# A two-dimensional Fourier transform followed by an MLP: the start of the program in finer pieces and another order

## The chip, the core and the metric

The kernel runs on one core of a Trainium2 chip. The metric is device time in microseconds (us) of one execution; three executions of the kernel before took 1763.95, 1764.96 and 1766.8 us, a median of 1764.96 us. The engines are named as the profile names them: PE is TensorE (matmul), DVE is VectorE, ACT is ScalarE, POOL is GpSimd, SP is SyncE, which here only issues DMAs.

## The reference

```python
def _attn_ref(x):                       # x: (8, 3008, 256)
    X = np.fft.fft(x, axis=1)
    X = np.fft.fft(X, axis=2)
    return X.real.astype(np.float32)
...
def _moe_ref(x, w_in, w_out, s, b):     # x: (24064, 256), w_in: (256, 2048), w_out: (2048, 256)
    h = x @ w_in
    r = np.maximum(h, 0.0)
    g = s * (r * r) + b
    return (g @ w_out).astype(np.float32)
```

The real part of a two-dimensional Fourier transform of each of eight batch items is taken; the result, as 24064 rows of 256 values, goes through an MLP with 2048 hidden units whose activation is the squared ReLU, scaled by `s` and shifted by `b`.

## The kernel before, in words

**The work.** The transform along the sequence is done as matmuls with tables of cosines and sines (`transform`, in two phases for a batch item); the transform along the 256 features is folded into the first weight matrix, so that the MLP's first layer reads the spectrum of the sequence directly. By symmetry only half of the columns is computed: 1506 for a batch item, in 3 blocks of 502. For every block the hidden units go through in 16 groups of 128. One group of one block is a **step**: 8 x 3 x 16 = 384 steps in all. A step has two halves.

- `first_layer` (L637): 6 matmuls into a two-bank PSUM tile `ab` (L643), then three VectorE instructions that add the term of the Nyquist feature (column `wny` times the row `ebc`) and form the sum and the difference for the two mirrored columns (L645 to L647, tile `h`), then on ScalarE ReLU, square (L648, L649) and a rounding cast to `gh` (L272), then on GpSimd the rest, `gl = h - gh` (L273). `split` (L270) is the helper that makes a high and a low part; every product of the kernel is made of three matmuls over such parts (high x high, high x low, low x high).
- `second_layer` (L659): 12 matmuls (L666) of `gh` and `gl` with the second weights `wo_h`, `wo_l` into four PSUM tiles `po`, which gather over the 16 steps of a block. `finish` (L671) scales them and writes them out.

**The start.** Before the first step can run, the first batch item has to be loaded, folded and transformed, and the weights have to be read. The letters of the table `START` each stand for one piece of a Python generator, which issues instructions up to its next `yield`:

- `x` and `y` (`load_first`, `load_second`): fold the eight tiles of the first item; the tables X_ON_VECTOR and Y_ON_VECTOR say for which tiles the work of a piece (L508 and L512, or L522 to L524) goes to VectorE instead of GpSimd.
- `s` and `u` (`transform(0, 0)`, `transform(0, 1)`): the two phases of its transform. A `pair` (L564) is 16 matmuls, then a copy out of PSUM (L579; by FIRST_COPIES_ON_SCALAR on ScalarE or VectorE) and VectorE sums (L580, L584, L585). Each phase ends in `store`, which casts the result into the blocks `spec_h` (ScalarE, L545) and takes the rest into `spec_l` (GpSimd, L547).
- `r`, `a`, `b`, `e`: the weights come as 64-bit floating-point numbers and are decoded in 16 parts. `r` issues the load of a part, `a` runs two ScalarE instructions (L308, L310), `b` three VectorE ones (L313 to L315), and `e` a GpSimd addition (L318), followed, for the eight parts of the second weights, by the `split` into `wo_h` (ScalarE) and `wo_l`.
- `w` (`fold_w_in`, L329): one of four foldings of the first weights: matmuls in float32 (L337; the profile counts eight), then a ScalarE copy of the Nyquist row (L341), the split into `wd_h` and `wd_l`, and two DMAs on SP (L343, L344) that write the row to DRAM and read it back as a column of `wny`. A folding serves four steps.
- `n` and `m` (`nyquist`): the transform of the Nyquist feature, stored to DRAM and read back as `ebc`.
- `t`: the load of the transform's tables.
- `L` and `S`: `first_layer` and `second_layer` of the next step. `l`, `v` and `o`: load and transform of the second batch item, for later steps.

**What sets the order.** The instructions of TensorE, VectorE, ScalarE and GpSimd are chained in the order in which they are issued (`_in_order`, L236): each engine executes its own list strictly in that order, and an instruction that waits holds up all behind it. DMAs on SP are outside of that chain. `START` covers 57 first halves and 54 second halves; from there on the table `BATCH` is run over and over, a string of letters for the 48 steps of one batch item and the load and transform of the next.

**Buffers.** The tiles `h`, `gh` and `gl` have three buffers each, `ab` two, the weight loads two (they use the buffers of the first two input tiles); at the start the input tiles 2 to 7 lie in the buffers of `gl` and `gh`, so that the first steps need these tiles folded.

Of the kernel before, what the change touches and what calls it, by code (L numbers as in the profile page):

```python
# [9 lines left out]
F32 = mybir.dt.float32  # L10
# [5 lines left out]
P = 128  # L16
NB, S, D, FF = 8, 3008, 256, 2048
# [4 lines left out]
G = 24  # L22
NL = 4 * G
NK = H + 2
NT = 502
# [11 lines left out]

LOWS_ON_VECTOR = (3, 5)  # L40
Y_ON_VECTOR = (0, 7)
X_ON_VECTOR = (1, 2, 3, 4, 6)
FIRST_COPIES_ON_SCALAR = (1, 2, 3, 4, 5)
COPIES_ON_SCALAR = ()
SUMS_ON_SCALAR = ()
LOADS = "xxfxxxwxwxx"
# [2 lines left out]
    ("in", 2, 1), ("out", 3), ("in", 3, 0), ("out", 4), ("in", 3, 1), ("out", 5), ("out", 6), ("out", 7),  # L49
)  # L50
START = (
# [6 lines left out]
)  # L58
BATCH = (
# [191 lines left out]
def kernel(ctx: ExitStack, tc: tile.TileContext, xq, xn, dft, turn, feat, w_in, w_out, s, b, out):  # L251
    nc = tc.nc
# [17 lines left out]
    def split(hi, lo, src, lo_engine):  # L270

        nc.scalar.copy(hi, src)  # L272
        lo_engine.tensor_sub(lo, src, hi.bitcast(F32))  # L273
# [9 lines left out]
    wny = const.tile([P, NJ], F32, name="wny")  # L283
# [19 lines left out]
    def decode(part, raw, aux):  # L303

        low, high = raw[:, :, 0], raw[:, :, 1]
        magnitude, bits = aux[:, 0], aux[:, 1]
        rest, w = magnitude.bitcast(F32), bits.bitcast(F32)
        nc.scalar.activation(rest, high.bitcast(F32), AF.Abs)  # L308

        nc.scalar.activation(low, low.bitcast(mybir.dt.uint32), AF.Copy, scale=2.0 ** -29)  # L310
        yield

        nc.vector.tensor_scalar(rest, rest, 2.0 ** -15, None, ALU.max)  # L313
        nc.vector.tensor_scalar(bits, magnitude, 3, 0x3FFFFFFF, ALU.logical_shift_left, ALU.bitwise_and)
        nc.vector.scalar_tensor_tensor(bits, high, -(1 << 30), bits, ALU.bitwise_and, ALU.bitwise_or)  # L315
        yield

        nc.gpsimd.tensor_add(bits, bits, low)  # L318
        if part[0] == "out":
            at = slice(2 * part[1], 2 * part[1] + 2)  # L320
            split(
                wo_h[:, at], wo_l[:, at], w.rearrange("p (j d) -> p j d", j=2),
                nc.vector if part[1] in LOWS_ON_VECTOR else nc.gpsimd,
            )
        else:
            halves[part[1:]] = w, rest
        yield

    def fold_w_in(f):  # L329

        (w0, row), (w1, _) = (halves[f, c] for c in range(2))
        row = row[0:1]
        at = slice(f * 512, (f + 1) * 512)
        ps = two_banks()
        for kind in range(2):
            for c, w in enumerate((w0, w1)):
                nc.tensor.matmul(  # L337
                    ps[:, kind], feat_sb[:, c, kind * P:(kind + 1) * P], w, start=c == 0, stop=c == 1
                )
        yield  # L340
        nc.scalar.copy(row, ps[0:1, 1])  # L341
        split(wd_h[:, :, at], wd_l[:, :, at], ps, nc.vector)
        nc.sync.dma_start(wny_dram[:, at], row)  # L343
        nc.sync.dma_start(wny[:, 4 * f:4 * f + 4], wny_dram[0, at].rearrange("(j p) -> p j", p=P))  # L344
        yield


# [289 lines left out]
    def first_layer(su, blk, j, ebc):  # L637
        mh, ml = block_of(su, blk)
        ps = two_banks()[:, :, :NT]
        fj = slice(j * P, (j + 1) * P)  # L640
        for kind in range(2):
            for i, (w, m) in enumerate(((wd_h, mh), (wd_h, ml), (wd_l, mh))):
                nc.tensor.matmul(ps[:, kind], w[:, kind, fj], m[:, kind], start=i == 0, stop=i == 2)  # L643
        h = act.tile([P, 2, NT], F32, name="h")
        nc.vector.scalar_tensor_tensor(h[:, 0], ebc, wny[:, j:j + 1], ps[:, 0], op0=ALU.mult, op1=ALU.add)  # L645
        sub(h[:, 1], h[:, 0], ps[:, 1])  # L646
        add(h[:, 0], h[:, 0], ps[:, 1])  # L647
        nc.scalar.activation(h, h, AF.Relu)  # L648
        nc.scalar.activation(h, h, AF.Square)  # L649
        gh = act.tile([P, 2, NT + 2], F32R, name="gh")  # L650
        gl = act.tile([P, 2, NT + 2], F32R, name="gl")
        if (su, blk) == (0, 0):

            nc.gpsimd.memset(gh[:, 0, NT:].bitcast(F32), 1.0)
            nc.gpsimd.memset(gl[:, 0, NT:].bitcast(F32), 0.0)  # L655
        split(gh[:, :, :NT], gl[:, :, :NT], h, nc.gpsimd)
        return gh, gl

    def second_layer(po, j, g, sums):  # L659
        gh, gl = g  # L660
# [76 lines left out]
    def go_on():  # L737
        for i in range(len(WORDS)):
            next(decoding[i])
            yield  # L740

    def fold_weights():
        for f in range(4):
            yield from fold_w_in(f)

    pending = []
    po = None
    ebc = None
    step = 0
# [1 line left out]
    def first():  # L751
        nonlocal ebc, step
        su, blk, j = step // (NBLK * NJ), step // NJ % NBLK, step % NJ
        step += 1
        if j == 0:
            ebc = small.tile([P, NT], F32, name="ebc")
            for ph in range(2):
                first, last = max(0, blk * NT - SPLIT * ph), min((blk + 1) * NT - SPLIT * ph, e_dram[ph].shape[1])
                if first < last:
                    at = first + SPLIT * ph - blk * NT  # L760
                    nc.sync.dma_start(
                        ebc[:, at:at + last - first], e_dram[ph][su, first:last].partition_broadcast(P)
                    )
        pending.append(((su, blk, j), first_layer(su, blk, j, ebc)))

    def second():
        nonlocal po
# [6 lines left out]

    work = {
        "t": tables(), "x": load_first(tiles), "y": load_second(tiles), "r": load_weights(), "a": begin_weights(),
        "b": go_on(), "e": go_on(), "w": fold_weights(),
        "n": nyquist(0, t_ny, room, room_r), "m": nyquist(1, t_ny, room, room_r),
        "s": transform(0, 0), "u": transform(0, 1), "l": load(1),
        "v": transform(1, 0), "o": transform(1, 1),  # L780
# [1 line left out]
    for what in START.split():  # L782
        if what == "L":
            first()
        elif what == "S":
            second()
        else:
            next(work[what])

    su = 1  # L790
    while step < NB * NBLK * NJ:
        work = {}
        if su < NB - 1:
            work = {"l": load(su + 1), "v": transform(su + 1, 0), "o": transform(su + 1, 1)}
        for what in BATCH.split():
            if what == "L" and step < NB * NBLK * NJ:
                first()
            elif what == "S" and pending:
                second()
            elif what in work:  # L800
                next(work[what])
        su += 1
# [35 lines left out]
```

## Time and profile before

| | us |
|---|---|
| median of three runs | 1764.96 |
| the profiled execution | 1766.39 |
| its span, first to last instruction | 1764.3 |
| PE busy in the span | 1683.20 |
| DVE busy | 1417.67 |
| ACT busy | 1285.81 |
| POOL busy | 953.85 |

A line of a timeline has the start in us, the duration in us, the engine, the line of the program, the operation, output and input tiles, and shapes; in square brackets stands how long the engine sat idle before it and what ended that. A line of a table of stages has the stretch, its length, and for each engine the busy us and the number of instructions, then the granted PE clock (1.00 is full speed), the share of DMA and the GB/s. A group's line has the count, the busy us, the mean in ns, and the idle time before.

### The profile page before, as it was taken

What the parts mean: (1) busy time and instruction counts of PE and PEld (TensorE: products, weight loads), DVE (VectorE), ACT (ScalarE), POOL (GpSimd) and SP (SyncE); (2) the same over time, 40 slices, a digit from 0 to 9 for tenths busy, and PEclk for the clock granted to TensorE, in tenths of its full rate; (3) what the DMA queues carried; (4) which work ended last, traced back from release to release, by engine and by line L of the source; (5) the groups of instructions that cost most, each with busy time, mean ns of one, the idle gap of its engine ahead of it and who ended that gap; (6) DMA issues with size and microseconds to landing.
All of it is one profiled execution on the core that took longest, in us unless ns stands there. A gap on an engine that the chain in (4) does not pass through costs nothing.

```text
span 1764.3 us, 21595 instructions
## 1 busy us (share of the span) xinstructions
PE 1683.2 (95%) x7537; PEld 1386.7 (79%) x7537; DVE 1417.7 (80%) x2145; ACT 1285.8 (73%) x1356; POOL 953.8 (54%) x550
## 2 busy tenths in 40 slices
PE   2687999999999999999999999999999999999998
PEld 1465778888888888888888888888888888888887
DVE  6779987889787997879878897879978798785554
ACT  2565677777778778777777777787787778787776
POOL 4555446555556555564565555565565555555554
PEclk9798999999999999999999999999999999999999
DMA  6321200011000200002000110002100020000000
GB/s 154 94 66 51 81 18 24 30 42 60 30 1 30 75 27 30 21 22 80 16 24 30 42 60 30 5 26 75 30 27 30 19 65 26 5 30 7 24 24 24
DMA packets 26100, 68.57 MB, mean 39 GB/s; under 512 B 5444, under 2 KB 10404, under 8 KB 25896
## 3 DMA queue, kind: packets, MB, share of 16 engines
q1 hardware_dynamic: 25464, 64.84, 11.9%
q0 software_dynamic: 528, 2.36, 0.6%
q8 instruction: 59, 0.97, 0.2%
q14 instruction: 49, 0.40, 0.1%
HBM read 42.46 MB, written 24.73 MB: 38 GB/s over the span
## 4 chain that ended last, share of the span: by engine, by line
PE 84%; DVE 8%; issue 1%; ACT 1%; DVEq 0%; ACTq 0%
PE po L666 54%; PE ab L643 27%; PE ab L573 2%; DVE h L645 1%; DVE h L646 1%; PE ab L574 1%; DVE h L647 1%; DVE xt L493 1%; DVE cs L498 1%; DVE xt L495 0%; DVE lf L352 0%; DVE xt L494 0%; DVE o L683 0%; DVE cs L497 0%; DVE fl L561 0%
## 5 line engine op out<-in xcount | busy, mean ns | idle before, releaser
L273 POOL TENSOR_TENSOR gl<-h,gh 128x1004 fp32r<-128x1004 f32 x384 | 842.2, 2193 | 749.6 <-ACT gh L272 530.0
L648 ACT ACTIVATE h<-h 128x1004 f32<-128x1004 f32 x384 | 400.3, 1042 | 362.7 <-DVE h L647 356.2
L666 PE MATMUL po<-gh,wo_h 128*128 128x502 f32 (+1 forms) x1536 | 484.8, 396 | 0.2
L645 DVE SCALAR_TENSOR_TENSOR h<-ebc,wny,ab 128x502 f32<-128x502 f32 x384 | 281.1, 732 | 246.9 <-PE ab L643 233.7
L666 PE MATMUL po<-gh,wo_l 128*128 128x502 f32 (+1 forms) x1536 | 477.8, 393 | 0.0
L666 PE MATMUL po<-gl,wo_h 128*128 128x502 f32 (+1 forms) x1536 | 476.9, 392 | 0.9 <-POOL gl L655 0.8
L649 ACT ACTIVATE h<-h 128x1004 f32<-128x1004 f32 x384 | 401.3, 1045 | 12.2
L272 ACT CAST gh<-h 128x1004 fp32r<-128x1004 f32 x384 | 397.4, 1035 | 12.4 <-PE po L666 0.3
L666 PEld LDWEIGHTS po<-gl,wo_h 128*128 128x128 f32 x1536 | 292.2, 190 | 61.6 <-POOL gl L655 1.8
L666 PEld LDWEIGHTS po<-gh,wo_l 128*128 128x128 f32 x1536 | 291.1, 189 | 61.9
L666 PEld LDWEIGHTS po<-gh,wo_h 128*128 128x128 f32 x1536 | 289.1, 191 | 60.3 <-DVE o L683 2.6
L643 PE MATMUL ab<-spec_h,wd_h 128*128 128x502 f32 x768 | 304.1, 396 | 27.9 <-DVE h L647 11.7
L643 PE MATMUL ab<-spec_h,wd_l 128*128 128x502 f32 x768 | 301.5, 393 | 3.1 <-DVE wd_l L273 3.1
L643 PE MATMUL ab<-spec_l,wd_h 128*128 128x502 f32 x768 | 300.0, 391 | 0.0
L647 DVE TENSOR_TENSOR h<-h,ab 128x502 f32<-128x502 f32 x384 | 260.5, 678 | 13.2
L646 DVE TENSOR_TENSOR h<-h,ab 128x502 f32<-128x502 f32 x384 | 260.2, 678 | 13.2
L643 PEld LDWEIGHTS ab<-spec_h,wd_h 128*128 128x128 f32 x768 | 146.0, 190 | 65.3 <-DVE h L647 16.8
L643 PEld LDWEIGHTS ab<-spec_h,wd_l 128*128 128x128 f32 x768 | 145.2, 189 | 33.6 <-DVE wd_l L273 3.5
L643 PEld LDWEIGHTS ab<-spec_l,wd_h 128*128 128x128 f32 x768 | 146.2, 190 | 28.9 <-issue 0.2
L573 PE MATMUL ab<-dft_sb,fh 96*128 96x192 f32 x256 | 63.5, 317 | 29.5 <-DMA dft_sb<-in_dft 19.2
L573 PEld LDWEIGHTS ab<-dft_sb,fh 96*128 96x128 f32 x256 | 51.6, 202 | 32.4 <-issue 19.2
L683 DVE TENSOR_SCALAR o<-po,sb_s,bias 128x502 f32<-128x502 f32 x94 | 68.8, 793 | 8.7 <-PE po L666 8.7
(93 smaller groups left out, 987.9 us busy)
## 6 DMA issues: line engine op xcount, KB each, us to landing
xt<-in_xq SPq DMA_DIRECT2D x64, 384.0 KB
out<-o SPq DMA_DIRECT2D x46, 502.0 KB
raw<-in_w_in SPq DMA_DIRECT2D x8, 512.0 KB
raw<-in_w_out SPq DMA_DIRECT2D x8, 512.0 KB
ebc<-e_dram SPq DMA_DIRECT2D x16, 251.0 KB
dft_sb<-in_dft POOLq DMA_DIRECT2D x2, 576.0 KB, 13.2
dft_sb<-in_dft POOLq DMA_DIRECT2D x1, 1152.0 KB, 7.4
ebc<-e_dram SPq DMA_DIRECT2D x8, 126.0 KB
```

What stands on the lines that cost most here:

```text
L272: nc.scalar.copy(hi, src)
L273: lo_engine.tensor_sub(lo, src, hi.bitcast(F32))
L493: add(t[:, 0::2], t[:, 0::2], t[:, 1::2])
L573: nc.tensor.matmul(ps[:, kind, i], fh[:, row, at], tab, start=True, stop=False)
L643: nc.tensor.matmul(ps[:, kind], w[:, kind, fj], m[:, kind], start=i == 0, stop=i == 2)
L645: nc.vector.scalar_tensor_tensor(h[:, 0], ebc, wny[:, j:j + 1], ps[:, 0], op0=ALU.mult, op1=ALU.add)
L646: sub(h[:, 1], h[:, 0], ps[:, 1])
L647: add(h[:, 0], h[:, 0], ps[:, 1])
L648: nc.scalar.activation(h, h, AF.Relu)
L649: nc.scalar.activation(h, h, AF.Square)
L666: nc.tensor.matmul(po[2 * pm + dh][:, :n], l[:, j, dh * P:(dh + 1) * P], r[:, pm, :n], start=start and first, stop=stop and last,)
L683: nc.vector.tensor_scalar(o[:, dh], po[2 * pm + dh][:, :NT], *args, ALU.mult, ALU.add)
```

## The change

**Finer pieces.** The decoding of a weight part has one `yield` more: the GpSimd addition stays with `e`, and the split of the second weights becomes a piece of its own, `f`. The folding of the first weights is cut into three pieces instead of two (the matmuls of the cosine half, those of the sine half, the split). `first_layer` becomes a generator as well: `L` ends with the cast to `gh`, and the subtraction that makes `gl` is a piece `G` of its own. For some of the steps of the first block the table LOWS_OF_STEPS_ON_VECTOR moves that subtraction from GpSimd to VectorE: its entries are 0 to 3, 8, 9, 10, 12 and 13, nine steps. In `BATCH` the subtraction follows the cast directly and stays on GpSimd, as before.

**Another placement.** The `wo_l` split is on VectorE for one part instead of two; the second-half folding `y` is on VectorE for five tiles instead of two; of the first item's eight copies out of PSUM three are on ScalarE instead of five.

**Another order.** `START` is a new string with the same numbers of steps (57 first halves, 54 second halves).

**The first Nyquist weights.** For the first folding, eight small products (weights as the stationary side, one column of the feature table as the moving side) give the Nyquist row directly as a column; one ScalarE copy of 128 x 4 values brings it to `wny`. The ScalarE copy of the row and the two DMAs through DRAM remain for the foldings 1 to 3.

```diff
-LOWS_ON_VECTOR = (3, 5)
-Y_ON_VECTOR = (0, 7)
-X_ON_VECTOR = (1, 2, 3, 4, 6)
-FIRST_COPIES_ON_SCALAR = (1, 2, 3, 4, 5)
+LOWS_OF_STEPS_ON_VECTOR = (0, 1, 2, 3, 8, 9, 10, 12, 13)
+LOWS_ON_VECTOR = (2,)
+Y_ON_VECTOR = (0, 1, 2, 3, 4)
+X_ON_VECTOR = (0, 1, 3, 4, 5)
+FIRST_COPIES_ON_SCALAR = (0, 1, 7)
...
 START = (
-    "n a x x x x n t y x b r t x x y s x a y e s s b s x s s e y r y y s a s n a s n s s t s s r e b y e w w a b "
...
+    "n t x a y x y n x x x r y s y s b t s x a e x s x b f r e a s b x s n f y s n a w s e w f b e s s f w r a m "
...
         nc.gpsimd.tensor_add(bits, bits, low)
+        yield
         if part[0] == "out":
...
+            if f == 0 and kind == 1:
+
+                column = ps_o.tile([P, 512], F32, name="po")
+                for i in range(4):
+                    for c, w in enumerate((w0, w1)):
+                        nc.tensor.matmul(
+                            column[:, i:i + 1], w[:, i * P:(i + 1) * P], feat_sb[:, c, P:P + 1],
+                            start=c == 0, stop=c == 1,
+                        )
+            yield
+        if f == 0:
+            nc.scalar.copy(wny[:, :4], column[:, :4])
+        else:
+            nc.scalar.copy(row, ps[0:1, 1])
         split(wd_h[:, :, at], wd_l[:, :, at], ps, nc.vector)
-        nc.sync.dma_start(wny_dram[:, at], row)
-        nc.sync.dma_start(wny[:, 4 * f:4 * f + 4], wny_dram[0, at].rearrange("(j p) -> p j", p=P))
+        if f > 0:
+            nc.sync.dma_start(wny_dram[:, at], row)
+            nc.sync.dma_start(wny[:, 4 * f:4 * f + 4], wny_dram[0, at].rearrange("(j p) -> p j", p=P))
...
-        split(gh[:, :, :NT], gl[:, :, :NT], h, nc.gpsimd)
-        return gh, gl
+        nc.scalar.copy(gh[:, :, :NT], h)
+        yield gh, gl
+        engine = nc.vector if su == blk == 0 and j in LOWS_OF_STEPS_ON_VECTOR else nc.gpsimd
+        engine.tensor_sub(gl[:, :, :NT], h, gh[:, :, :NT].bitcast(F32))
+        yield
...
-        pending.append(((su, blk, j), first_layer(su, blk, j, ebc)))
+        lows.append(first_layer(su, blk, j, ebc))
+        pending.append(((su, blk, j), next(lows[-1])))
...
+        elif what == "G":
+            next(lows.pop(0))
```

**The order on VectorE around the first steps.** This is VectorE's list before, from behind the first step's three instructions on `h` to the first instruction of the second step (`h_482`); `xt` is an input tile being folded by a piece `y`, `aux` are weights being decoded, `wd_l` is the low part of the second folding.

```order
L522 TENSOR_TENSOR xt_122<-xt_122 96x256
L523 TENSOR_TENSOR cs_102<-xt_122 96x128
L524 TENSOR_TENSOR cs_102<-xt_122 96x128
L313 TENSOR_SCALAR aux_388<-aux_388 128x512
L314 TENSOR_SCALAR aux_388<-aux_388 128x512
L315 SCALAR_TENSOR_TENSOR aux_388<-raw_366,aux_388 128x512
L313 TENSOR_SCALAR aux_419<-aux_419 128x512
L314 TENSOR_SCALAR aux_419<-aux_419 128x512
L315 SCALAR_TENSOR_TENSOR aux_419<-raw_417,aux_419 128x512
L273 TENSOR_TENSOR wd_l_90<-ab_457,wd_h_89 128x2x512
L412 TENSOR_TENSOR room_r_99<-room_98,room_r_99 96x320
L645 SCALAR_TENSOR_TENSOR h_482<-ebc_422,wny_91,ab_475 128x502
```

And this is VectorE's list in the changed kernel, from the first step's first instruction (here `h_469`) on; `h_490` and `h_512` belong to the second and the third step.

```order
L661 SCALAR_TENSOR_TENSOR h_469<-ebc_460,wny_91,ab_462 128x502
L662 TENSOR_TENSOR h_469<-h_469,ab_462 128x502
L663 TENSOR_TENSOR h_469<-h_469,ab_462 128x502
L661 SCALAR_TENSOR_TENSOR h_490<-ebc_460,wny_91,ab_483 128x502
L662 TENSOR_TENSOR h_490<-h_490,ab_483 128x502
L663 TENSOR_TENSOR h_490<-h_490,ab_483 128x502
L661 SCALAR_TENSOR_TENSOR h_512<-ebc_460,wny_91,ab_505 128x502
L662 TENSOR_TENSOR h_512<-h_512,ab_505 128x502
L663 TENSOR_TENSOR h_512<-h_512,ab_505 128x502
L675 TENSOR_TENSOR gl_476<-h_469,gh_475 128x2x502
```

The three first steps now stand one behind another; the second `wd_l`, which stood between the first and the second step, has moved ahead of the first, and the first step's `gl`, which was on GpSimd, follows the third step's `h`.

**The order on ScalarE at the same place.** Before, ScalarE's list goes on from the first step's square (`h_431`) like this; `wo_h` are the high parts of second weights, each directly behind its GpSimd addition, and `wd_h` is the second folding.

```order
L649 ACTIVATE h_431<-h_431 128x1004
L272 CAST gh_437<-h_431 128x2x502
L272 CAST wo_h_92<-aux_388 128x512
L341 COPY cs_102<-ab_457 1x512
L272 CAST wd_h_89<-ab_457 128x2x512
L272 CAST wo_h_92<-aux_419 128x512
```

In the changed kernel the list runs from the two `wo_h` casts to the third step's `h_512`.

```order
L274 CAST wo_h_92<-aux_352 128x512
L274 CAST wo_h_92<-aux_383 128x512
L310 ACTIVATE aux_457<-raw_448 128x512
L312 ACTIVATE raw_448<-raw_448 128x512
L664 ACTIVATE h_469<-h_469 128x1004
L665 ACTIVATE h_469<-h_469 128x1004
L672 CAST gh_475<-h_469 128x2x502
L664 ACTIVATE h_490<-h_490 128x1004
L665 ACTIVATE h_490<-h_490 128x1004
L672 CAST gh_496<-h_490 128x2x502
L664 ACTIVATE h_512<-h_512 128x1004
```

The two `wo_h` casts and the second `wd_h` have moved from behind the first step's `gh` to ahead of the first step, and the casts of the three first steps follow one another.

More of the change, by code (lines that the diff above doesn't have):

```diff
@@ L339, in fold_w_in @@
                 )
-        yield
-        nc.scalar.copy(row, ps[0:1, 1])
+            if f == 0 and kind == 1:
[11 more added lines that the diff above has]
+            nc.scalar.copy(row, ps[0:1, 1])
         split(wd_h[:, :, at], wd_l[:, :, at], ps, nc.vector)
-        nc.sync.dma_start(wny_dram[:, at], row)
-        nc.sync.dma_start(wny[:, 4 * f:4 * f + 4], wny_dram[0, at].rearrange("(j p) -> p j", p=P))
+        if f > 0:
+            nc.sync.dma_start(wny_dram[:, at], row)
+            nc.sync.dma_start(wny[:, 4 * f:4 * f + 4], wny_dram[0, at].rearrange("(j p) -> p j", p=P))
         yield
@@ L744, in fold_weights @@
             yield from fold_w_in(f)
-    pending = []
+    pending, lows = [], []
     po = None
@@ L776 @@
         "t": tables(), "x": load_first(tiles), "y": load_second(tiles), "r": load_weights(), "a": begin_weights(),
-        "b": go_on(), "e": go_on(), "w": fold_weights(),
+        "b": go_on(), "e": go_on(), "f": go_on(), "w": fold_weights(),
         "n": nyquist(0, t_ny, room, room_r), "m": nyquist(1, t_ny, room, room_r),
@@ L797 @@
                 first()
+                next(lows.pop(0))
             elif what == "S" and pending:
```

11 rows, old and new, of the table START are left out of this document.

## The prediction

> **What bounds the kernel now.** I read the page's busy lines and slices first, then the busy time by stage, then who waited for whom in the start, then the timeline at the longest waits. The page:
>
> ```profile
> PE 1683.2 (95%) x7537; PEld 1386.7 (79%) x7537; DVE 1417.7 (80%) x2145; ACT 1285.8 (73%) x1356; POOL 953.8 (54%) x550
> PE   2687999999999999999999999999999999999998
> ```
>
> TensorE is the bound as a whole, but in its first four slices of 44 us it is busy for less than 90%. The table of stages, with busy us of each engine, shows where its 81 us of idle time lie:
>
> ```profile
> 0.00:30.00 30.00, 3.21 (x14) 3.00 (x14) 18.57 (x50) 6.05 (x13) 9.94 (x17) 1.00 0.89 227
> 30.00:62.00 32.00, 18.08 (x72) 12.05 (x72) 26.55 (x44) 9.85 (x23) 20.24 (x27) 0.75 0.30 71
> 62.00:97.00 35.00, 23.32 (x92) 17.05 (x91) 26.35 (x40) 25.09 (x36) 18.31 (x19) 0.84 0.25 71
> 97.00:123.00 26.00, 21.17 (x107) 16.38 (x104) 15.46 (x25) 13.65 (x23) 13.66 (x14) 0.87 0.27 82
> 123.00:190.00 67.00, 52.03 (x196) 38.01 (x195) 63.21 (x87) 41.36 (x50) 32.10 (x36) 0.89 0.18 52
> 190.00:222.00 32.00, 32.00 (x135) 26.18 (x134) 31.34 (x49) 21.54 (x22) 16.29 (x8) 0.96 0.27 82
> 222.00:247.00 25.00, 24.93 (x118) 20.76 (x117) 20.15 (x33) 19.68 (x21) 12.04 (x6) 1.00 0.06 17
> 247.00:265.00 18.00, 15.61 (x62) 12.52 (x61) 16.32 (x20) 11.70 (x12) 8.12 (x4) 0.91 0.06 14
> 265.00:400.00 135.00, 133.93 (x612) 111.46 (x611) 107.71 (x169) 101.76 (x107) 76.25 (x42) 1.00 0.10 31
> 400.00:1600.00 1200.00, 1199.15 (x5446) 997.34 (x5445) 1008.73 (x1519) 916.77 (x941) 664.10 (x343) 1.00 0.11 34
> ```
>
> From 265 us on TensorE is idle for 1.9 us of 1335: whatever reaches that point earlier ends earlier by the same amount. Ahead of it TensorE lacks 26.8, 13.9, 11.7, 4.8, 15.0, 0, 0.1 and 2.4 us in the eight stages. In the fifth, VectorE is busy for 63.2 of 67 us and in the sixth for 31.3 of 32: there VectorE is the bound. But in the four stages ahead, VectorE itself is idle for 11.4, 5.5, 8.7 and 10.5 us. So the start is a chain of waits up to 123 us, then VectorE's backlog, then TensorE. The next view, who waited for whom up to 265 us (total, times, longest), says what VectorE waited for:
>
> ```profile
> ACT wo_h L272 <- POOL aux L318: 13.7, 5, 3.6
> PE ab L643 <- DVE wd_l L273: 12.7, 2, 9.6
> DVE xt L507 <- DMA xt<-in_xq: 8.2, 5, 4.6
> DVE t L580 <- ACT t L579: 6.9, 4, 2.6
> DVE wd_l L273 <- ACT wd_h L272: 6.7, 1, 6.7
> DVE wo_l L273 <- ACT wo_h L272: 6.7, 1, 6.7
> ```
>
> Of the 24.6 us between 30 and 123 us, three rows hold 20.3. The timeline at the longest one reads as a chain:
>
> ```profile
> 69.58 2.13 POOL L273 TENSOR_TENSOR gl<-h,gh 128x1004 fp32r<-128x1004 f32 x1 [9.40 <-ACT gh L272]
> 71.66 1.27 POOL L318 TENSOR_TENSOR aux<-aux,raw 128x512 int32<-128x512 int32 x1
> 72.97 0.62 ACT L272 CAST wo_h<-aux 128x512 fp32r<-128x512 f32 x1 [3.47 <-POOL aux L318]
> 73.97 1.00 ACT L272 CAST wd_h<-ab 128x1024 fp32r<-128x1024 f32 x1
> 75.00 1.23 DVE L273 TENSOR_TENSOR wd_l<-ab,wd_h 128x1024 fp32r<-128x1024 f32 x1 [6.73 <-ACT wd_h L272]
> 76.28 0.79 PE L643 MATMUL ab<-spec_h,wd_h 128*128 128x502 f32 x1 [9.62 <-DVE wd_l L273]
> ```
>
> The first step's `gl` on GpSimd delays an addition of the weights, this holds up ScalarE's queue at `wo_h`, the `wd_h` behind it is late, VectorE stands at `wd_l`, and TensorE at the second step. Nothing in it is needed in that order but `gl`.
>
> **The change part by part.** The point to which I carry the sum is the first instruction on `h` of step 33 and the TensorE wait that follows, the last long one:
>
> ```profile
> 257.96 0.73 DVE L645 SCALAR_TENSOR_TENSOR h<-ebc,wny,ab 128x502 f32<-128x502 f32 x1
> 260.17 0.50 PE L643 MATMUL ab<-spec_h,wd_h 128*128 128x502 f32 x1 [2.39 <-DVE h L647]
> ```
>
> Up to it VectorE was busy for 201.6 us by 247 (the first seven stages) and idle for 45.4; the eighth stage adds 1.7 idle by 265, so about 47 up to step 33. The same steps, loads and transforms stand ahead of step 33 in both orders (but for one `fl` that falls just behind it, which I leave in), so VectorE's work changes only by what changes engines. The prices, from groups up to 265 us:
>
> ```profile
> L273 POOL TENSOR_TENSOR gl<-h,gh 128x1004 fp32r<-128x1004 f32 x33 | 72.5, 2198 | 81.0 <-ACT gh L272 73.0 <-DVE h L645 4.2 <-DVE lf L359 2.1
> L561 DVE TENSOR_TENSOR fl<-lf,fh 96x1024 fp32r<-96x1024 f32 x3 | 3.7, 1221 | 3.3 <-ACT fh L558 3.3
> L561 DVE TENSOR_TENSOR fl<-cs,fh 96x512 fp32r<-96x512 f32 x3 | 3.7, 1219 | 1.4 <-ACT fh L558 1.4
> L561 DVE TENSOR_TENSOR fl<-lf,fh 96x512 fp32r<-96x512 f32 x3 | 2.0, 679 | 0.0
> L522 POOL TENSOR_TENSOR xt<-xt 96x256 f32<-96x256 f32 x6 | 5.8, 974 | 0.0
> L523 POOL TENSOR_TENSOR cs<-xt 96x128 f32<-96x128 f32 x6 | 3.3, 552 | 0.5
> L522 DVE TENSOR_TENSOR xt<-xt 96x256 f32<-96x256 f32 x2 | 0.8, 414 | 0.0
> L273 POOL TENSOR_TENSOR wo_l<-aux,wo_h 128x512 fp32r<-128x512 f32 x6 | 7.8, 1297 | 6.3 <-ACT wo_h L272 6.3
> L273 DVE TENSOR_TENSOR wo_l<-aux,wo_h 128x512 fp32r<-128x512 f32 x2 | 1.4, 686 | 6.7 <-ACT wo_h L272 6.7
> L579 DVE COPY t<-ab 128x384 f32<-128x384 f32 x5 | 2.7, 548 | 0.0
> ```
>
> *Nine `gl` on VectorE.* No `gl` ran there. The nearest row is `fl` over 1024 values, the same subtraction of a rounded copy, 1.22 us. The two rows over 512 show a further 0.54 us when something is in the way (1.219 against 0.679). So 11.0 to 15.9 us; I take 12.0. GpSimd loses 9 x 2.198 = 19.8 us.
>
> *Three more `y` tiles on VectorE.* 0.414 us for the first instruction and at most that for each half-width one: 2.7 to 3.7, I take 3.0. GpSimd loses 3 x (0.974 + 2 x 0.552) = 6.2 us.
>
> *Two more copies, one `wo_l` less.* 2 x 0.548 - 0.686 = 0.4 us; GpSimd gains 1.3. `x` stays at five tiles of eight: nothing.
>
> VectorE's added work is thus 15.4 us (14.1 to 20.0). **This term speaks against the change: VectorE is the bound from 123 to 222 us, and alone it makes the kernel 15 us slower.**
>
> *The idle time.* In the new order the first steps' `h` stand together, the second `wd_l` stands ahead of them, and no `wo_h` cast stands between the first step's `gh` and what follows it: the chain above is gone, with VectorE's 6.7. The other 6.7 is the same figure once more, a `wo_h` that ScalarE could not begin before GpSimd's addition; as a piece `f` of its own it stands after other work. The 6.9 at `t` are ScalarE copies that VectorE waits for; two of five become VectorE's own. A `G` on VectorE waits for its `gh`: ScalarE needs three casts of some 1.0 us, and behind the first step VectorE has two more steps to do, each with three instructions of 0.7, so the first one finds its `gh` nearly done. Of the 24.6 us I keep 6 and count 18.6 saved. In the first 30 us the loads rule (8.2 us of waits for `xt`); the earlier `y` pieces fill a part of that: 2 saved. After 190 us VectorE was idle for 0.7, 4.9 and 1.7 us because TensorE had become the bound; with VectorE later relative to TensorE these go too: 6.5 saved. Together 27, of 47. Its ends are 12 (only the two chained waits go) and 36 (only the loads' waits stay).
>
> *GpSimd's lighter load.* VectorE's instructions stretch beside GpSimd's. The same operation on the same shape:
>
> ```profile
> L508 DVE TENSOR_TENSOR xt<-xt 96x256 f32<-96x256 f32 x5 | 2.2, 449 | 0.2
> L494 DVE TENSOR_TENSOR xt<-xt 96x256 f32<-96x256 f32 x8 | 9.1, 1142 | 0.3
> ```
>
> The first row lies in the first 30 us with GpSimd busy for a third, the second in the later stages beside `gl`: 0.69 x 8 = 5.5 us more. GpSimd loses 19.8 + 6.2 - 1.3 = 24.7 of the 110.5 us that it works up to 222 us, 22%. One group of eight then gives 1.2; I take 3 for all groups, between 0 and 8.
>
> A rule weighs on both terms. The Trainium skill, "SBUF — State Buffer", section "Who interferes with whom", says that a VectorE instruction with two SBUF inputs and a GpSimd instruction that reads SBUF exclude each other, and that whoever comes later waits for the other's end. Both forms of `gl` are of that kind by it; the trace agrees so far as 1142 ns stands against 449. By that rule each of the nine could wait for the rest of a GpSimd instruction, and the sum below would be -5 instead of -15; the second rival works this out.
>
> *The Nyquist column.* Eight products replace a ScalarE copy and two DMAs. TensorE loads weights of that form in 0.25 us:
>
> ```profile
> L337 PEld LDWEIGHTS ab<-cs,feat_sb 128*128 128x128 f32 x24 | 5.9, 252 | 11.8 <-issue 5.8 <-POOL gl L655 5.7
> ```
>
> At up to two loads each that is 2 to 4 us of TensorE, in a stretch where it is idle for 13.9 of 32; if that cover were gone, 4 us. SP loses two issues, which moves the loads of weights behind them ahead; the view of waits has no row of VectorE waiting for `wny`, so I count nothing, either way.
>
> *TensorE and the rest.* Its matmuls are the same; `BATCH` is unchanged and its `gl` stays on GpSimd. SP's 14 weight loads come earlier, as the buffers are free earlier; they are needed one by one later. Between 265 and 400 us VectorE has 27 us to spare, so the 15 added us do not come back there.
>
> Sum up to step 33: +15.4 work, -27 idle, -3 stretching = **-14.6 us**, about -15. Against the profiled execution: span 1764.3 to about 1749. That execution took 1766.39, its span and 2.1 around it, 1.4 above the median of the runs, so the median of 1764.96 becomes **1750**.
>
> **The rivals.** *A larger gain.* VectorE keeps only the loads' waits, 36 saved, and stretches 5 less: 15.4 - 36 - 5 = -26, so 1739. For it: three rows hold most of the idle time. Against: every new order has waits of its own. Chance 0.13.
>
> *The `gl` collide with GpSimd.* If each of the nine waits for half of a GpSimd instruction of 2.2 us, 10 us come on top: -14.6 + 10 = -5, so 1760. For it: 1142 against 449. Against: in the stages in question GpSimd has fewer `gl` left to collide with. Chance 0.12.
>
> *Slower: VectorE stands at the `G`.* VectorE's list is strict; behind a `G` whose `gh` is late stand the next steps' `h`, which TensorE and ScalarE wait for. ScalarE needs 3.1 us for a step, so a `G` one step behind its `L` waits for up to 3 us: 9 x 3 = 27, and -14.6 + 27 = +12, so 1777. It decides from 1.6 us a `G` on. For it: `G` 5 to 14 stand among decodings of weights that ScalarE also has to do. Against: the table puts two or three pieces between most `L` and their `G`. Chance 0.11.
>
> *No change.* The time saved before step 12 is given back: 12 us of idle time saved and 3 less stretching make 15.4 - 15 = 0, so 1765. Chance 0.09.
>
> **How the numbers follow.** The forecast of 1750 has a chance of 0.55, with 1744 to 1757 as its own range. A change of 0.2% is 3.5 us, about what a measurement of this kernel can tell. Faster by more than that (below 1761.4) are the forecast, the larger gain and two thirds of the collision: 0.55 + 0.13 + 0.08 = 0.76. Within it lie the rest of the collision and the no-change case, less a little that falls outside: 0.12. Slower: 0.12. For 8 in 10 the range leaves out the slower case and half of the largest gains: 1738 to 1766.
>
> **What would show it.** Right: by 123 us VectorE idle for about 20 instead of 36 us; step 12's `h` (154.25 us before) near 130, step 33's `h` near 243; no wait of 6 us of VectorE for ScalarE; GpSimd's busy time up to 222 us about 25 us less; `gl` on VectorE at 1.2 to 1.6 us.
>
> ```profile
> 154.25 0.73 DVE L645 SCALAR_TENSOR_TENSOR h<-ebc,wny,ab 128x502 f32<-128x502 f32 x1
> ```
>
> Wrong: waits of 2 to 3 us in front of VectorE's `gl`, `gl` there at over 2 us, or TensorE idle again after 265 us.

## The result and the profile after

| | before, us | after, us |
|---|---|---|
| median (four runs each) | 1765.88 (1763.95 to 1766.93) | 1727.00 (1726.05 to 1727.97) |
| ratio, 95% interval | | 0.9781 [0.9764, 0.9798] |
| span of the profiled execution | 1764.3 | 1725.8 |
| PE busy / idle in the span | 1683.2 / 81.1 | 1674.5 / 51.3 |
| first `h` of step 1, 12, 33 | 62.22, 154.25, 257.96 | 59.27, 119.00, 211.21 |

The kernel became 38.9 us faster; the forecast was 1750, a gain of 15, and the range ended at 1738. The sign and the place were right, the size was not. The page of the changed kernel, busy lines, TensorE's slices and its granted clock:

```profile
PE 1674.5 (97%) x7553; PEld 1380.8 (80%) x7553; DVE 1407.2 (82%) x2164; ACT 1284.7 (74%) x1354; POOL 932.1 (54%) x533
PE   3799999999999999999999999999999999999998
PEclk9899999999999999999999999999999999999999
```

TensorE is now below 90% in two slices of 43 us instead of four. Of the 38.5 us of span, 29.8 are TensorE's idle time and 8.7 its busy time, although it has 16 more instructions: it ran less of its work at a lowered clock. VectorE's busy time fell too, by 10.5 us, although work was added to it. That is the first sign of where the forecast went wrong. The same stages as before (stretch, length, busy us and count of PE, PEld, DVE, ACT, POOL, then clock, DMA share, GB/s):

```profile
0.00:30.00 30.00, 7.44 (x44) 6.46 (x45) 23.24 (x62) 8.05 (x17) 6.76 (x13) 1.00 0.91 227
30.00:62.00 32.00, 21.23 (x72) 12.96 (x71) 29.54 (x59) 16.18 (x35) 18.07 (x20) 0.84 0.43 116
62.00:97.00 35.00, 31.31 (x128) 22.98 (x128) 33.08 (x51) 29.00 (x35) 20.02 (x30) 0.95 0.26 78
97.00:123.00 26.00, 24.46 (x130) 18.52 (x129) 25.41 (x40) 20.47 (x26) 11.22 (x15) 1.00 0.24 73
123.00:190.00 67.00, 65.46 (x300) 53.76 (x298) 63.57 (x105) 53.20 (x62) 39.08 (x30) 1.00 0.19 58
190.00:222.00 32.00, 32.00 (x146) 26.62 (x145) 29.25 (x49) 22.64 (x23) 15.47 (x8) 1.00 0.17 45
265.00:400.00 135.00, 131.54 (x588) 108.77 (x587) 118.40 (x175) 99.35 (x102) 71.97 (x36) 1.00 0.14 43
```

VectorE is idle for 11.7 us of the first 123, where it was idle for 36.1. From 97 us on TensorE lacks only 1.5 us in each of the next two stages: it is the bound some 90 us earlier than before, where VectorE still ruled from 123 to 222. The granted clock tells the same: 0.95 and then 1.00, where it was 0.84 to 0.89 up to 190 us. Who waited for whom up to 265 us, VectorE's rows and below them TensorE's only long row after 265 us (total, times, longest):

```profile
DVE h L661 <- PE ab L659: 9.5, 7, 2.0
DVE h L661 <- POOL spec_l L563: 4.1, 2, 3.1
DVE xt L523 <- DMA xt<-in_xq: 3.6, 3, 1.7
DVE wd_l L275 <- ACT wd_h L274: 2.4, 3, 1.0
...
PE ab L659 <- DVE h L663: 6.3, 4, 2.5
```

The waits of 6.7 us for ScalarE are gone. VectorE's largest wait is now for TensorE, which is what a kernel bound by TensorE should show. The timeline of VectorE at the place where the chain of waits stood before:

```profile
63.45 0.73 DVE L661 SCALAR_TENSOR_TENSOR h<-ebc,wny,ab 128x502 f32<-128x502 f32 x1
64.21 0.68 DVE L662 TENSOR_TENSOR h<-h,ab 128x502 f32<-128x502 f32 x1
64.92 0.68 DVE L663 TENSOR_TENSOR h<-h,ab 128x502 f32<-128x502 f32 x1
65.52 1.29 DVE L675 TENSOR_TENSOR gl<-h,gh 128x1004 fp32r<-128x1004 f32 x1
...
211.21 0.73 DVE L661 SCALAR_TENSOR_TENSOR h<-ebc,wny,ab 128x502 f32<-128x502 f32 x1
```

No row has a wait in brackets: the third step's `h`, right behind those of the first two (from 59.27 and 61.37 on), then the first step's `gl`, whose `gh` is done. So far the forecast is confirmed. What it missed stands in the groups. The same operations up to 265 us, before:

```profile
L352 DVE SCALAR_TENSOR_TENSOR lf<-uv,turn_sb 96x256 f32<-96x256 f32 x8 | 8.4, 1100 | 0.0
L313 DVE TENSOR_SCALAR aux<-aux 128x512 f32<-128x512 f32 x10 | 7.0, 696 | 0.2 <-ACT aux L308 0.2
L495 DVE TENSOR_TENSOR xt<-xt 96x256 f32<-96x256 f32 x8 | 5.3, 660 | 0.0
```

And after:

```profile
L675 DVE TENSOR_TENSOR gl<-h,gh 128x1004 fp32r<-128x1004 f32 x9 | 10.8, 1207 | 0.0
L368 DVE SCALAR_TENSOR_TENSOR lf<-uv,turn_sb 96x256 f32<-96x256 f32 x8 | 3.4, 473 | 0.0
L315 DVE TENSOR_SCALAR aux<-aux 128x512 f32<-128x512 f32 x10 | 5.1, 507 | 0.0
L510 DVE TENSOR_TENSOR xt<-xt 96x256 f32<-96x256 f32 x8 | 5.2, 652 | 0.3
L511 DVE TENSOR_TENSOR xt<-xt 96x256 f32<-96x256 f32 x8 | 3.3, 414 | 0.0
```

Apart from the `gl`, which are new on VectorE, these instructions did not change; they got shorter. L510 is the line shown in the prediction as L494, at 1142 ns; L352, L313 and L495 are now L368, L315 and L511. Each instruction had been stretched, by something that no row of waits names.

To weigh this, VectorE's time ahead of step 33 is divided into three: **work** (every instruction at the shortest duration that the same operation on the same tiles and shape has in the traces of the kernel before and of the changed one), **stretch** (what each took above that) and **idle** (the brackets). Consecutive rows overlap a little, so the three add up to 7 to 9 us more than the time.

| VectorE ahead of step 33, us | work | stretch | idle | first `h` of step 33 |
|---|---|---|---|---|
| before | 176.5 | 46.9 | 41.6 | 258.0 |
| after | 188.9 | 20.4 | 10.8 | 211.2 |
| change (forecast) | +12.4 (+15.4) | -26.5 (-3) | -30.8 (-27) | -46.8 (-14.6) |

### The profile page after: what moved, and what is told of

Read it like the earlier page. It is cut to its first block, busy times and chain, and to the rows that moved or that the text cites. A ratio compares the mean times of both kernels' runs of the same rounds, so it can differ in the third digit from the quotient of the medians.

```text
span 1725.8 us, 21616 instructions
## 1 busy us (share of the span) xinstructions
PE 1674.5 (97%) x7553; PEld 1380.8 (80%) x7553; DVE 1407.2 (82%) x2164; ACT 1284.7 (74%) x1354; POOL 932.1 (54%) x533
## 4 chain that ended last, share of the span: by engine, by line
PE 90%; DVE 7%; ACT 1%; issue 1%; DMA 1%; POOL 1%; SPq 0%; DVEq 0%; ACTq 0%; POOLq 0%
PE po L685 58%; PE ab L659 29%; PE ab L589 2%; PE ab L590 1%; DVE h L661 1%; DVE h L662 1%; DVE h L663 1%; DMA xt<-in_xq 1%; PE ab L340 1%; DVE xt L509 0%; DVE gl L675 0%; DVE xt L511 0%; DVE fl L577 0%; POOL gl L675 0%; DVE lf L368 0%
## 5 line engine op out<-in xcount | busy, mean ns | idle before, releaser
L675 POOL TENSOR_TENSOR gl<-h,gh 128x1004 fp32r<-128x1004 f32 x375 | 822.2, 2193 | 708.0 <-ACT gh L672 470.9
L702 DVE TENSOR_SCALAR o<-po,sb_s,bias 128x502 f32<-128x502 f32 x94 | 68.8, 794 | 8.3 <-PE po L685 8.3
L563 POOL TENSOR_TENSOR spec_l<-o,spec_h 128x368 fp32r<-128x368 f32 (+3 forms) x80 | 63.9, 819 | 17.0 <-ACT spec_h L561 16.4
```

The source lines that it names most:

```text
L563: nc.gpsimd.tensor_sub(lo, src, hi.bitcast(F32))
L675: engine.tensor_sub(gl[:, :, :NT], h, gh[:, :, :NT].bitcast(F32))
L702: nc.vector.tensor_scalar(o[:, dh], po[2 * pm + dh][:, :NT], *args, ALU.mult, ALU.add)
```

## The experiments

**Two theories.** *A:* the finer pieces and their order make the gain, by waits that go. *B:* GpSimd's lighter load makes it: nine `gl` and three `y` tiles leave GpSimd, and VectorE stretches less beside it. All ratios are against the kernel before, measured beside each.

| run | edit | median, us | ratio [95%] | step 33 | work, stretch, idle |
|---|---|---|---|---|---|
| e1 | no `gl` on VectorE | 1735.61 | 0.9831 [0.9817, 0.9846] | 220.2 | 178.6, 33.9, 15.5 |
| e2 | old placements | 1736.17 | 0.9834 [0.9820, 0.9849] | 223.1 | 186.5, 25.8, 19.4 |
| e3 | both of these | 1738.21 | 0.9844 [0.9828, 0.9861] | 226.7 | 175.7, 33.1, 24.9 |
| e4 | e1, `G` tied to `L` | 1759.64 | 0.9969 [0.9956, 0.9982] | 244.8 | 178.6, 25.7, 48.1 |
| e5 | no piece `f` | 1748.91 | 0.9907 [0.9891, 0.9923] | 236.6 | 190.8, 17.6, 38.5 |
| e6 | Nyquist through memory | 1726.62 | 0.9779 [0.9762, 0.9797] | 210.9 | |
| e7 | before, nine `gl` on VectorE | 1794.20 | 1.0164 [1.0148, 1.0180] | 283.6 | 188.2, 42.0, 64.0 |
| e10 | before, GpSimd reads nothing for `gl` | 1749.95 | 0.9914 [0.9897, 0.9930] | 243.6 | 177.2, 22.4, 51.4 |
| e11 | sixteen `gl` on VectorE | 1749.83 | 0.9909 [0.9894, 0.9923] | 237.2 | 197.0, 18.2, 30.7 |
| e12 | four `gl` on VectorE | 1727.45 | 0.9784 [0.9769, 0.9798] | 214.9 | 183.9, 26.5, 13.7 |

### e1, e2, e3: the order without the new engines

```diff
-LOWS_OF_STEPS_ON_VECTOR = (0, 1, 2, 3, 8, 9, 10, 12, 13)    # e1, e3
+LOWS_OF_STEPS_ON_VECTOR = ()
-LOWS_ON_VECTOR = (2,)                                       # e2, e3
-Y_ON_VECTOR = (0, 1, 2, 3, 4)
-X_ON_VECTOR = (0, 1, 3, 4, 5)
-FIRST_COPIES_ON_SCALAR = (0, 1, 7)
+LOWS_ON_VECTOR = (3, 5)
+Y_ON_VECTOR = (0, 7)
+X_ON_VECTOR = (1, 2, 3, 4, 6)
+FIRST_COPIES_ON_SCALAR = (1, 2, 3, 4, 5)
```

> The changed kernel with all nine gl of the first block back on GpSimd, at the same places of the order. Changed kernel 1727.0, before 1765.9. Theory A (the order in finer pieces does it: waits are gone and VectorE's instructions no longer meet GpSimd's): each of the nine is about 1 us longer (2.19 against 1.21) and hidden behind other steps, so 1727 to 1733, VectorE's stretched time ahead of step 33 stays near 20 us. Theory B (GpSimd's lighter load does it): 19.8 us go back to GpSimd, the stretched time goes back up by 10 us or more and the time to 1740 to 1750.

> The changed kernel with the old tables for y, x, the copies out of PSUM and wo_l (three y tiles back on GpSimd, five copies on ScalarE, two wo_l on VectorE); gl stays on VectorE. Theory A: 1727 to 1733, since VectorE loses 3.4 us of work and gains some waits. Theory B: GpSimd gets 6 us back in the first 60 us, the first step starts later by about as much, 1733 to 1740.

> Both undone: every instruction on the engine that it had before, only the new order, the finer pieces and the Nyquist column are left. Theory A: at least 25 of the 39 us stay, 1728 to 1740. Theory B: less than half stays, 1746 to 1760.

The order, the pieces and the column alone (e3) take 1765.7 to 1738.2: 27.5 of the 38.9 us, theory A's share. Of VectorE's time that is 16.7 idle and 13.8 stretch: the order alone also shortens instructions. The nine `gl` are worth 8.6 us with the new placements (e1 against the changed kernel) and 2.0 without them (e2 against e3); the placements 9.2 with the nine `gl` and 2.6 without. Both together are worth 11.2. Theory B holds for that part alone. VectorE's groups up to 265 us in e1, against the changed kernel's 507 and 473 ns:

```profile
L315 DVE TENSOR_SCALAR aux<-aux 128x512 f32<-128x512 f32 x10 | 8.8, 881 | 1.2 <-ACT aux L310 1.2
L368 DVE SCALAR_TENSOR_TENSOR lf<-uv,turn_sb 96x256 f32<-96x256 f32 x8 | 5.3, 709 | 0.0
```

With the nine `gl` back on GpSimd the same instructions are stretched again. The nine cost VectorE 10.3 us of work and save it 13.5 of stretch and 4.7 of idle time. Of the three times, e3's lies where theory A put it and e2's where theory B did; e1's lies between the two, with the stretch that theory B expected.

### e4 and e5: the pieces tied together again

```diff
         pending.append(((su, blk, j), next(lows[-1])))      # e4, on top of e1
+        next(lows.pop(0))
...
         elif what == "G":
-            next(lows.pop(0))
+            pass
...
         nc.gpsimd.tensor_add(bits, bits, low)               # e5
-        yield
...
+        elif what == "f":
+            pass
```

> The changed kernel with all gl on GpSimd and each directly behind its cast in the order, as before (the piece G is tied to L again). To be held against the run with all gl on GpSimd and G apart. Theory A: G as a piece of its own keeps gl out of the way of GpSimd's additions for the weights and of VectorE's SBUF instructions, so tying it costs 5 to 15 us and stretched time comes back. Theory B: GpSimd's load is the same in both, so within 2 us of it.

> The changed kernel with the split of the second weights tied to the GpSimd addition again (no piece f). Theory A, in the form of the prediction: ScalarE again waits for GpSimd's addition at each of eight wo_h (2 to 3.5 us each as before), which delays what stands behind it on ScalarE, 5 to 10 us in all: 1732 to 1737. If VectorE's list is not behind these casts: within 2 us of 1727.

Tying `G` to `L` costs 24.0 us against e1. Tying the split of the second weights to GpSimd's addition costs 21.9 us against the changed kernel. Both are more than the 5 to 15 and 5 to 10 us that were expected. Both are idle time of VectorE (+32.6 and +27.7), and stretch even falls, where it was expected to come back in e4. Waits in e4, up to 265 us, VectorE's and two on the way to them:

```profile
DVE wd_l L275 <- ACT wd_h L274: 18.4, 4, 8.2
DVE cs L315 <- ACT cs L310: 12.5, 2, 7.1
...
POOL gl L675 <- ACT gh L672: 66.7, 28, 7.9
...
PEld ab L340 <- POOL cs L320: 13.8, 2, 13.3
```

The longest wait for `wd_h` ends a chain: a `gl` stands on GpSimd for 7.8 us, the addition of weights behind it is late, TensorE's folding (L340) waits for that until 97.4 us, and `wd_h` and `wd_l` come behind it. It is the chain of the forecast without its station at `wo_h`.

In e5 (its lines stand one lower) ScalarE's queue stands at `wo_h` again, as in the chain that the prediction showed:

```profile
ACT wo_h L274 <- POOL aux L320: 14.7, 5, 4.7
...
DVE h L660 <- PE ab L658: 22.1, 8, 9.3
DVE wd_l L275 <- ACT wd_h L274: 10.8, 4, 5.1
```

So the chain that the forecast named is what the pieces take away, and in this order each of the two cuts is needed. The order was made for pieces that stand apart; what the best order of tied ones would take was not run.

### e6: the Nyquist weights through memory

```diff
-            if f == 0 and kind == 1:
+            if False:
...
-        if f == 0:
+        if False:
...
-        if f > 0:
+        if True:
```

> The changed kernel with the first Nyquist weights through DRAM, as before. If the prediction was right to count nothing for the column: within 2 us of 1727. If the round trip is now late for the first step, which stands 3 us earlier: 3 to 5 us more, 1730 to 1732, with VectorE waiting for a DMA ahead of the first step.

1726.62 against 1727.00, with ranges that overlap: the column by products is worth nothing here, as forecast.

### e7: the nine `gl` on VectorE in the old order

```diff
-        split(gh[:, :, :NT], gl[:, :, :NT], h, nc.gpsimd)
+        split(gh[:, :, :NT], gl[:, :, :NT], h, nc.vector if su == blk == 0 and j in (0, 1, 2, 3, 8, 9, 10, 12, 13) else nc.gpsimd)
```

> The kernel before with the nine gl on VectorE, each directly behind its cast, in the old order. The rival of the prediction (VectorE's strict list stands at the gl until ScalarE's three casts are done, 3 us each): slower than before by 5 to 20 us, 1771 to 1785. Theory B (a lighter GpSimd gives the time): faster by 5 us or more, under 1760.

28 us slower than before, where 5 to 20 were expected. The group of `gl` up to 290 us:

```profile
L273 DVE TENSOR_TENSOR gl<-h,gh 128x1004 fp32r<-128x1004 f32 x9 | 10.8, 1205 | 32.3 <-ACT gh L272 32.3
```

VectorE stands for 3.6 us at each `gl`. This is the slower rival's mechanism, and it decides where that rival put it, above 1.6 us. In the changed kernel the same group has 0.0 us of waits, because `START` puts 5 to 19 letters between the `L` and the `G` of each of the nine steps.

### e9: the two engines side by side

Behind the changed kernel's work six stages of eight VectorE instructions each were added: three forms, each alone and with a GpSimd subtraction for every one.

```diff
+    def stage_of(vector, beside):
+        nc.scalar.copy(va, vb)
+        nc.scalar.copy(pm[:, :, :NT], vb)
+        nc.scalar.copy(ga[:, :, :NT], vb)
+        for i in range(8):
+            vector()
+            if beside:
+                nc.gpsimd.tensor_sub(gd[:, :, :NT], ga[:, :, :NT], gb[:, :, :NT])
...
+        sub(vd, va, vb)
...
+        sub(vd, va, pm[:, :, :NT])
...
+        nc.vector.tensor_scalar(vd, va, 2.0, None, ALU.mult)
```

> The changed kernel with six short stages added behind its end, 8 instructions of VectorE over 1004 values each: a subtraction of two SBUF operands, one of an SBUF and a PSUM operand, and a multiplication by a constant, each once alone and once beside 8 subtractions of two SBUF operands on GpSimd. If the two engines exclude each other only where both read two SBUF operands or VectorE runs a constant form: the first and the third go from about 1.2 and 0.7 us alone to 2 to 3 us beside GpSimd, the second stays at about 1.2. If they only share bandwidth: all rise a little. If the stretched time of before had another cause: none rises.

VectorE's groups in the stretches 1723 to 1735 (two SBUF operands, alone), 1735 to 1758 (the same beside GpSimd) and 1770 to 1782 (one operand in PSUM, beside GpSimd), the last form's durations (shortest, median, longest), and rows of the timeline of the second stage, in which instructions that stand back to back are one row:

```profile
L846 DVE TENSOR_TENSOR vd<-va,vb 128x1004 f32<-128x1004 f32 x8 | 9.6, 1204 | 3.4 <-ACT va L837 3.2
...
L846 DVE TENSOR_TENSOR vd<-va,vb 128x1004 f32<-128x1004 f32 x8 | 21.5, 2689 | 1.4 <-ACT va L837 1.1
...
L849 DVE TENSOR_TENSOR vd<-va,ab 128x1004 f32<-128x1004 f32 x8 | 9.6, 1199 | 2.3 <-ACT ab L838 2.0
...
L852 DVE TENSOR_SCALAR vd<-va x16: 682/2572/2664, 1782.4 to 1810.0; 128x1004 f32<-128x1004 f32 x16
...
1735.77 2.44 DVE L846 TENSOR_TENSOR vd<-va,vb 128x1004 f32<-128x1004 f32 x2 [1.15 <-ACT va L837]
1737.73 2.64 POOL L843 TENSOR_TENSOR gd<-ga,gb 128x1004 f32<-128x1004 f32 x1 [19.26 <-ACT ga L839]
1738.25 9.62 DVE L846 TENSOR_TENSOR vd<-va,vb 128x1004 f32<-128x1004 f32 x3
```

The mean of 2689 ns mixes two kinds. VectorE's first two subtractions began before GpSimd's first one and took 1.2 us each; the six that began beside GpSimd took 3.18 each. Beside a GpSimd subtraction VectorE's thus takes 1.98 us longer; with one operand in PSUM it takes nothing longer. The constant form's stage alone wasn't clean, as GpSimd still worked off the stage ahead of it. Over its two stages, the nine instructions beside GpSimd's took 2.48 to 2.66 us and the other seven 0.68: again up to 1.98 more.

So one subtraction on GpSimd costs VectorE up to 1.98 us where it meets an instruction that works in SBUF alone, and nothing beside the instructions on `h`, L702 or L595, which read PSUM. The 13.5 us of stretch between e1 and the changed kernel are on average 1.5 for each of the nine `gl`, within that price. This is the rule that the prediction weighed (the Trainium skill, "SBUF — State Buffer", section "Who interferes with whom"); the trace agrees with it.

### e10: GpSimd writes but reads nothing

```diff
-        split(gh[:, :, :NT], gl[:, :, :NT], h, nc.gpsimd)
+        if su == 0 and 16 * blk + j < 33:
+            nc.scalar.copy(gh[:, :, :NT], h)
+            nc.scalar.copy(gl[:, 0, :1], h[:, 0, :1])
+            nc.gpsimd.memset(gl[:, :, :NT].bitcast(F32), 0.0)
+            nc.gpsimd.memset(gl[:, :, :NT].bitcast(F32), 0.0)
+        else:
+            split(gh[:, :, :NT], gl[:, :, :NT], h, nc.gpsimd)
```

> The kernel before, old order, but for the first 33 steps GpSimd doesn't subtract: it writes constants into gl twice (two memsets, behind ScalarE's cast and a small ScalarE write into the same tile), so that the low part of the hidden values is left out there. GpSimd stands at the same places and waits for the same casts, but reads no SBUF. If VectorE's stretched time ahead of step 33 (47 us before) comes from GpSimd reading SBUF beside it, it falls to 20 to 30 us, and the time falls by 10 to 25 us, to 1740 to 1755. If it comes from something else (semaphores, the order alone), it stays above 40 us and the time within 5 us of before.

GpSimd's and VectorE's groups up to 265 us:

```profile
L660 POOL MEMSET gl<- 128x1004 f32 x33 | 31.6, 957 | 1.9
L659 POOL MEMSET gl<- 128x1004 f32 x33 | 31.0, 939 | 77.4 <-ACT gl L658 77.4
...
L494 DVE TENSOR_TENSOR xt<-xt 96x256 f32<-96x256 f32 x8 | 3.4, 421 | 0.3
L352 DVE SCALAR_TENSOR_TENSOR lf<-uv,turn_sb 96x256 f32<-96x256 f32 x8 | 3.4, 472 | 0.0
```

In the old order, with GpSimd busy for 1.90 us a step instead of 2.20, the groups of 1142 and 1100 ns fall to 421 and 472. Stretch falls from 46.9 to 22.4 and the kernel gains 16 us. It is GpSimd's reading of SBUF that stretches VectorE's instructions with two operands in SBUF: ahead of step 33 some forty of them ran beside memsets alone, and none took more than 15 ns above its shortest. Constant forms are another case: of the five beside memsets alone, four took 0.2 to 0.7 us longer. By the same section of the Trainium skill a GpSimd instruction that only writes does not block one of VectorE with two SBUF inputs; these rows agree. Idle time rose by 9.8 us, so a part of the freed time turned into waits: ahead of step 33, VectorE's for TensorE at `h` grew from 2.9 to 8.3 us, and the old chain's two waits, 6.7 us each before, stayed at 6.9 and 7.3.

### e11 and e12: sixteen and four

```diff
-LOWS_OF_STEPS_ON_VECTOR = (0, 1, 2, 3, 8, 9, 10, 12, 13)
+LOWS_OF_STEPS_ON_VECTOR = tuple(range(16))                  # e11
+LOWS_OF_STEPS_ON_VECTOR = (0, 1, 2, 3)                      # e12
```

> The changed kernel with all 16 gl of the first block on VectorE instead of nine. If each gl costs VectorE 1.2 us there and 1.5 us beside it on GpSimd, the seven more are about even for VectorE: 1725 to 1729. If the seven steps were left out of the table since their casts are late at that place of the order, VectorE waits at them, 1 to 3 us each: 1730 to 1745.

> The changed kernel with only the gl of the steps 0 to 3 on VectorE. Nine were worth 8.6 us. If the worth is one of stretched time, spread evenly over the nine, 5 of 9 of it goes: 1730 to 1734. If it is one of the first steps' delay alone: within 2 us of 1727.

All sixteen cost 22.8 us against nine, above both ranges that were expected, though stretch falls by another 2.2. The waits of TensorE and VectorE up to 265 us in e11:

```profile
PE po L685 <- DVE gl L675: 17.4, 5, 10.9
...
DVE h L661 <- PE ab L659: 13.5, 8, 4.9
DVE h L661 <- POOL gl L675: 6.9, 3, 5.4
```

VectorE's list is strict, and a `gl` that lies late in it holds up TensorE's second layer. Four do as well as nine, 1727.45 against 1727.00, with ranges that overlap. The stretch of the other five came back (26.5 against 20.4) and step 33 comes 3.7 us later, but the end does not: a part of the nine's lead isn't used. No version that ran beats the changed kernel by more than the measurement tells.

## Why the prediction was wrong

**The failed step is "GpSimd's lighter load": "One group of eight then gives 1.2; I take 3 for all groups, between 0 and 8."** The term measured 26.5 us. Two faults made it small. First, it scaled one group by GpSimd's loss of load, 22%, and guessed the rest, where the trace of before already held 46.9 us of stretch, to be summed row by row against the shortest row of each form (46.8 by the shortest rows of that trace alone). Second, it took stretching as proportional to GpSimd's busy time. It depends on what lies beside what: e3 leaves every `gl` on GpSimd and still loses 13.8 us of stretch. The time that GpSimd's two-operand instructions ahead of step 33 spent beside VectorE instructions without a PSUM operand, added up from the timelines, was about 66 us before, 52 in e3 and 36 after; beside those with one it was 46, 58 and 63. Instruction by instruction the two traces leave no other source: ahead of step 33 no VectorE instruction with an operand in PSUM, and none without a two-operand GpSimd instruction beside it, took more than 20 ns above its shortest. All but some 1.5 us of the stretch, before and after, lies on the rest.

**The idle time** was right: -30.8 for -27, by the chain that was named (e4, e5). By 123 us VectorE was idle for 11.7 instead of 36.1 (20 was forecast), and no wait for ScalarE exceeds 1.0 us. With the stretch gone as well, step 12 came at 119.0 where 130 was forecast, and step 33 at 211.2 where 243 was.

**The added work** was near: +12.4 for +15.4. `gl` took 1.207 us each where 1.33 was taken.

**GpSimd's 25 us** were right for the same work: ahead of step 33 its busy time went from 129.2 to 103.5. As the prediction put the sign, by the clock "up to 222 us", it failed: 110.5 and 110.6, because the changed kernel is further on by then.

**"Whatever reaches that point earlier ends earlier by the same amount"** held only in part: step 33 came 46.8 us earlier, the end 38.5. Busy time of the engines ahead of and behind step 33's first `h`, of the kernel before:

```profile
0.00:258.00 258.00, 185.52 (x769) 142.02 (x769) 211.45 (x331) 144.21 (x189) 129.23 (x128) 0.90 0.29 79
258.00:1764.00 1506.00, 1497.69 (x6768) 1244.69 (x6768) 1206.23 (x1816) 1141.60 (x1167) 824.62 (x422) 1.00 0.10 32
```

And of the changed one:

```profile
0.00:211.20 211.20, 171.10 (x762) 132.41 (x763) 195.35 (x348) 138.94 (x184) 103.53 (x110) 0.97 0.35 96
211.20:1725.00 1513.80, 1503.41 (x6792) 1248.38 (x6791) 1211.82 (x1817) 1145.72 (x1171) 828.60 (x424) 1.00 0.10 32
```

Behind step 33's `h` TensorE still has 24 instructions and 5.7 us more to do than before, and 2.1 us more idle time: VectorE had run ahead of it, and its lead is no gain where TensorE is the bound. The idle time is of the kind that the prediction excluded ("the 15 added us do not come back there") and named as a sign of being wrong: after 265 us TensorE now waits for VectorE's `h` for 6.3 us, where it was 1.8. The longest wait, with what stands before it on VectorE:

```profile
319.70 2.55 DVE L600 TENSOR_TENSOR o<-x,t 128x384 f32<-128x384 f32 x1
322.17 0.55 DVE L601 TENSOR_TENSOR o<-x,t 128x384 f32<-128x384 f32 x1
...
324.85 0.50 PE L659 MATMUL ab<-spec_h,wd_h 128*128 128x502 f32 x1 [2.50 <-DVE h L663]
```

The first row takes 2.55 us where the like one behind it takes 0.55: a stretched instruction again, with a `gl` on GpSimd beside it from 319.68 to 321.84 us.

**TensorE's clock** was not in the sum. Its busy time fell by 8.7 us with 16 instructions added. As that time lies ahead of step 33, it is taken as a part of why the end could follow VectorE so far, not as a gain on top; that is argued, not shown.

**The rivals.** The larger gain named waits; it was half right, since the idle time stayed within its 36, but the 5 us of stretching in its sum were too few as well. The collision of `gl` did not come: 1.207 us each is what e9 shows for one alone. The same exclusion that was counted against the change worked for it. The slower rival is real in the old order (e7) and absent from the new one; the "two or three pieces" that were held against it are 5 to 19 letters of `START`. "No change" fell.

**What stays open.** Why `gl` and the placements are worth 8.6 and 9.2 us with each other and 2.0 and 2.6 alone isn't settled; both shift what lies beside what, and no run separates that. The table shows only where it lies: of the 6.6 us that the two are worth beyond their sum, VectorE's stretch accounts for 6.2 (33.1 and 20.4 against 33.9 and 25.8). The share of the clock in the end's 38.5 us was not measured by itself.

## What to carry to other kernels

Ahead of a forecast, divide the bounding engine's time into work at the shortest duration of each form, stretch above it, and idle time; here the stretch was larger than the idle time and stood in no row of waits. When VectorE and GpSimd work side by side, put GpSimd's two-operand reads beside VectorE's PSUM instructions, and move a subtraction to VectorE only where its input is long done. When a piece of work hands over between engines that run strict lists, cut it at the handovers: in this order, undoing either of the two cuts cost over 20 us.

## What the hardware showed that was not expected

- A VectorE subtraction 128x1004 in SBUF took 1204 ns alone and 3182 to 3186 beside GpSimd's; with one operand in PSUM, 1200 and 1199. A constant form of the same size, which reads one tile only, took 682 to 684 ns alone and up to 2664 beside. GpSimd's own subtraction took 2.31 us beside the form with PSUM and 3.14 beside the one with two SBUF operands.
- GpSimd's memset of 128x1004 took 0.94 to 0.96 us and left VectorE's two-operand rows near their shortest (means of 421 and 472 ns, where the shortest are 408 and 468).
- TensorE's granted clock stood at 0.84 to 0.89 between 62 and 190 us before, and at 0.95 and then 1.00 after, where its gaps had closed.
